# A third raw weight buffer, and another order of the vector work around each step of a gated layer

## The chip, the cores and the metric

The kernel runs on one core of a Trainium2 chip, as one launch. The metric is the device time of one execution in microseconds (us), lower is better. Five engines of the core work here, each on its own instruction stream and strictly in order: PE (TensorE, the matmuls), DVE (VectorE), ACT (ScalarE), POOL (GpSimd) and SP (SyncE), which only issues the transfers. They meet through semaphores, so an instruction that waits holds up everything behind it on its engine.

## The reference

Windowed attention, then a gated layer with SiLU, then a gated layer with a cosine, over 2304 tokens:

```python
attn = softmax(mask(scale * q @ k.T + bias))       # window of 128, 8 heads of 64, 4 sequences of 576
x = concat_heads(attn @ v)                         # [2304, 512]
g = x @ w_gate                                     # 512 x 1536
y = ((g * (1 / (1 + exp(-g)))) * (x @ w_val)) @ w_out   # 1536 x 512
h = y @ w_in2                                      # 512 x 2048
out = (h * cos(h)) @ w_out2                        # 2048 x 512
```

The five weight matrices come as 64-bit floats, q, k and v as 32-bit floats.

## The kernel before

Each matmul operand is held as a high and a low part whose sum is the number, and a product is three matmuls (`mm3`: high·high, high·low, low·high; lines L80, L81, L82). Three phases follow one another. The first does the attention and, as filler, the first 384 hidden columns of the first layer. **The second, which the change touches, does the other 1152 hidden columns of the first layer**, and beside that turns 64-bit weights into high and low parts: those of the first layer for its own later use, those of the second layer for the DRAM tensors `wid` and `wod`. The third does the second layer, which is written with seven products in the place of eight for every 2x2 block of tiles and therefore needs sums of weight blocks (`sm`).

The second phase is a loop of 54 steps. A step is a block of 128 hidden columns (f) and a block of 384 tokens (tb). The hidden blocks go in groups: [3], [4, 5], [6, 7], [8, 9], [10, 11], and for every group the loop runs over the six token blocks and, within them, over the blocks of the group. Step k issues on PE `begin(k)`, which is 12 matmuls for the gate, 12 for the value, and `second(k-2)`, 12 matmuls with `w_out` for the step two before: 36 matmuls in all. The gate bank goes through SiLU on ACT (L984) into `s`, DVE multiplies it by the value bank (L986), `split` makes the high part `uh` on ACT (L993) and the low part `ul` on DVE (L994). The four output banks of `second` are added over a group, and after the last block of the group four DVE adds (L1017) empty them into `acc`; they are posted and come out of `flush` in the next step. The output banks come from a pool of five, so with four in use the next group finds one free bank and must wait for an add for each of the other three.

The weight work is the class `Pipe`. It takes 56 raw tiles (128 x 512 numbers of 64 bits, 512 KB each) through these stages: a transfer into a `stage` tile (L91, L96), issued by SP; two ACT scalings of its upper and lower words (L909, L910), in `scalar`; three DVE operations on the bits (L871, L872, L873) and a POOL add (L875), in `vector`, after which the stage tile is free; then an ACT cast to the high part and a POOL subtract for the low part (L926 and L927 for the first layer, L946 and L947 for the stash, which goes out to DRAM by L952 and L954 from `start`). Tiles of the kind "b" also need four DVE operations for the sums (L891 to L894). Nothing decides the order at run time: every engine's stream is the order in which this loop writes it. In `load` a tile's transfer is written as soon as the add of the tile two before it has been:

```python
while len(self.stages) < min(len(self.todo), self.added + 2):
    self.stages.append(self.todo[len(self.stages)][2]())
```

In a step the order is: `split(k-1)`, `flush` (the bank-emptying adds), `start`, `vector` for the tiles scaled in the step before, `load`, `begin(k)`, then `scalar`, then `second(k-2)`. `scalar` begins one tile, in three steps of ten two.

Of the kernel before, what the change touches and what calls it, by code (L numbers as in the profile page):

```python
# [9 lines left out]
F32 = mybir.dt.float32  # L10
F32R = mybir.dt.float32r
U32 = mybir.dt.uint32
AF = mybir.ActivationFunctionType
ALU = mybir.AluOpType
# [14 lines left out]
def kernel(  # L29
# [12 lines left out]
    nc = tc.nc  # L42
# [20 lines left out]
    xs, cv = ExitStack(), ExitStack()  # L63
    x_pool = xs.enter_context(tc.tile_pool(name="xhl", bufs=1, reuse_waits="tile"))
    wa2_p = ctx.enter_context(tc.tile_pool(name="wa2", bufs=3, side="right", reuse_waits="tile"))
    wa_p = cv.enter_context(tc.tile_pool(name="wa", bufs=6, side="right", reuse_waits="tile"))
    stage_p = cv.enter_context(tc.tile_pool(name="stage", bufs=2, side="right", reuse_waits="tile"))
    cvt = ExitStack()
    conv_p = cvt.enter_context(tc.tile_pool(name="conv", bufs=2, side="right", reuse_waits="tile"))

    xh = x_pool.tile([128, KD, NT], F32R, name="xh")
# [4 lines left out]
    def f32(ap):  # L76
        return ap.bitcast(F32)
# [5 lines left out]

    wide = w_gate.dtype != F32

    def load_stage(src, f, column):
        st = stage_p.tile([128, 512, 2 if wide else 1], U32 if wide else F32, tag="st", name="st")
        src = src.bitcast(U32) if wide else src
        if column:
            n = src.shape[1] // (src.shape[1] // (256 if wide else 128))  # L90
            nc.sync.dma_start(  # L91
                out=st.rearrange("p (k c) t -> p k (c t)", k=KD),
                in_=src[:, f * n:(f + 1) * n].rearrange("(k p) c -> p k c", p=128),
            )
        else:
            nc.sync.dma_start(out=st.rearrange("p c t -> p (c t)"), in_=src[f * 128:(f + 1) * 128, :])  # L96
        return st
# [99 lines left out]
    def flush():  # L197
        for _ in range(len(post)):
            post.popleft()()
# [624 lines left out]
    class Pipe:  # L824
# [3 lines left out]
        def __init__(self):  # L828
            self.todo = []
            for i in range(1, len(groups1)):  # L830
                new = []
                for f in groups1[i]:
                    pool = wa_p if i % 2 else (wa2_p if f == groups1[i][0] else wb_p)
                    for nm, src, col in (("g", w_gate, True), ("v", w_val, True), ("o", w_out, False)):
                        new.append(("w", (i, nm, f), lambda src=src, f=f, col=col: load_stage(src, f, col), pool))
                old = self.stash(2 * i - 4) + self.stash(2 * i - 3) if i > 1 else []
                self.todo += old[:4] + new + old[4:]
            self.todo += self.stash(6) + self.stash(7)
            self.stages, self.begun, self.ct = [], 0, {}
            self.added = self.done = 0  # L840
            self.logic, self.sums, self.parts, self.outs = [], [], deque(), []
            self.kept, self.freed = {}, set()

        def stash(self, p):
            def col(f):
                return lambda: load_stage(w_in2, f, True)

            def row(f):
                return lambda: load_stage(w_out2, f, False)
            return [("a", p, col(2 * p), None), ("b", p, col(2 * p + 1), None),  # L850
                    ("o", 2 * p, row(2 * p), None), ("o", 2 * p + 1, row(2 * p + 1), None)]

# [6 lines left out]
            self.outs = []  # L859

        def load(self):
            while len(self.stages) < min(len(self.todo), self.added + 2):
                self.stages.append(self.todo[len(self.stages)][2]())

        def vector(self):
            for n in self.logic:
                kind, key = self.todo[n][:2]
                st, ct = self.stages[n], self.ct[n]
                if wide:
                    ti = ct.bitcast(U32)  # L870
                    nc.vector.tensor_scalar(ct, ct, LEAST_HIGH, GREATEST_HIGH, ALU.max, ALU.min)  # L871
                    nc.vector.tensor_scalar(ti, ti, 3, None, ALU.logical_shift_left)  # L872
                    nc.vector.scalar_tensor_tensor(out=ti, in0=st[:, :, 1], scalar=0x80000000, in1=ti,  # L873
                                                   op0=ALU.bitwise_and, op1=ALU.bitwise_or)
                    nc.gpsimd.tensor_tensor(out=ti, in0=ti, in1=st[:, :, 0], op=ALU.add)  # L875
                self.added += 1
                self.stages[n] = None
                if kind == "b":
                    self.sums.append((n, 1))
                else:  # L880
                    self.parts.append((n, 0))
            self.logic = []
            later = []
            for n, wait in self.sums:
                if wait:
                    later.append((n, 0))
                    continue
                p = self.todo[n][1]
                a, b = self.kept.pop(p), self.ct[n]
                m = stash_m.tile([128, 4, 256], F32, tag="sm", name="sm")  # L890
                nc.vector.tensor_tensor(out=m[:, 1], in0=b[:, 0:256], in1=b[:, 256:512], op=ALU.add)  # L891
                nc.vector.tensor_tensor(out=m[:, 2], in0=a[:, 0:256], in1=b[:, 0:256], op=ALU.subtract)
                nc.vector.tensor_tensor(out=m[:, 0], in0=m[:, 1], in1=a[:, 0:256], op=ALU.subtract)
                nc.vector.tensor_tensor(out=m[:, 3], in0=a[:, 256:512], in1=m[:, 0], op=ALU.subtract)  # L894
                self.freed.add(n - 1)
                self.kept[n] = m
                self.parts.extendleft([(n, 3), (n, 2), (n, 1)])
            self.sums = later

        def scalar(self, count, ready):  # L900

# [13 lines left out]
            used = 0  # L915
            for _ in range(len(self.parts)):
                n, part = self.parts.popleft()
                kind, key, _, pool = self.todo[n]
                if kind == "w" and not ready(key[0]) or kind != "w" and used == 4:
                    self.parts.append((n, part))  # L920
                    continue
                ct = self.ct[n]
# [11 lines left out]
                if kind == "o":  # L934
                    d = wod[key]
                elif part in (1, 2):
                    src = self.kept[n][:, 2 * part - 2:2 * part].rearrange("p s c -> p (s c)")
                    d = wid[key][:, 2 * part:2 * part + 2]
                elif part == 3:
                    src, w, d = ct[:, 256:512], 256, wid[key][:, 6]  # L940
                else:
                    d = wid[key][:, 0:2]
                    self.kept[key] = ct
# [45 lines left out]
    def split(k):  # L989
        u = state[k]  # L990
        hi = u_p.tile([128, BW], F32R, tag="uh", name="uh")
        lo = u_p.tile([128, BW], F32R, tag="ul", name="ul")
        nc.scalar.copy(out=hi, in_=u)  # L993
        nc.vector.tensor_tensor(out=lo, in0=u, in1=f32(hi), op=ALU.subtract)  # L994
        state[k] = (hi, lo)

    out_ps = {}

# [93 lines left out]
    nc.sync.dma_start(out=acc[:, :, NT - HT:], in_=y1d[:, :, NT - HT:].rearrange("k p t -> p k t"))  # L1092
    fa.close()
    cvt.close()
    ct_p = cv.enter_context(tc.tile_pool(name="cs", bufs=5, side="right", reuse_waits="tile"))
    stash_m = cv.enter_context(tc.tile_pool(name="sm", bufs=1, side="right", reuse_waits="tile"))
    stash_s = cv.enter_context(tc.tile_pool(name="ss", bufs=4, side="right", reuse_waits="tile"))
    s_p2 = sb.enter_context(tc.tile_pool(name="s2", bufs=3, reuse_waits="tile"))
    u_p = sb.enter_context(tc.tile_pool(name="u", bufs=2, reuse_waits="tile"))

    K = len(steps)
    RATEP = 1.3
    begins = {}
    for k, (i, tb, f) in enumerate(steps):
        begins.setdefault(i, k)
    CLOSE = begins[LAST] + 2 * len(groups1[LAST]) + 1
    xt_ops = []

    def work(k, count):
        pipe.start()  # L1110
        pipe.vector()
        pipe.load()
        return lambda: pipe.scalar(count, lambda i: k >= begins[i - 1] + 2)

    for k in range(K + 1):
        if k < K:
            i, tb, f = steps[k]
            while not all((i, nm, f) in weights for nm in "gvo"):
                work(k, 1)()
        if 0 <= k - 1 < K:  # L1120
            split(k - 1)
        flush()
        if k == CLOSE:
            while not pipe.idle():
                work(k, 2)()
            cv.close()
            xta = pre.enter_context(tc.tile_pool(name="xta", bufs=1, side="right", reuse_waits="tile"))
            wsp[0] = pre.enter_context(tc.tile_pool(name="ws", bufs=7, side="right", reuse_waits="tile"))
            load_ws(7)
        if k == CLOSE + 1:  # L1130
            xt_ops = make_xt(0, xta, acc[:, :, 0:SB])
        after = work(k, int((k + 1) * RATEP) - int(k * RATEP)) if k < CLOSE else None
        if k < K:
            begin(k)
        if after:
            after()
        for op in xt_ops[:4]:
            op()
        xt_ops = xt_ops[4:]
        if 0 <= k - 2 < K:  # L1140
            second(k - 2)
# [199 lines left out]
```

## Time and profile before

| | us |
|---|---|
| device time, median of 3 executions | 1170.75 (1166.32 to 1173.18) |
| the profiled execution, device time | 1169.83 |
| its span | 1168.1 |
| first phase, up to the first multiply of the second phase that follows a wait for a raw tile | 312.17 |
| second phase from there to the end of its weight work (44 steps) | 409.37 |
| rest of the second phase, to its last multiply (8 steps) | 50.40 |
| third phase | 396.16 |

The profiled execution is 0.92 us (0.1%) faster than the median and 1.7 us longer than its span. Engine times are busy times within a stretch; the granted clock of PE is a share of its full speed of 2.4 GHz, and a PE that is busy at half clock still counts as busy. Waits are idle times of an engine, put down to what ended them.

### The profile page before, as it was taken

What the parts mean: (1) busy time and instruction counts of PE and PEld (TensorE: products, weight loads), DVE (VectorE), ACT (ScalarE), POOL (GpSimd) and SP (SyncE); (2) the same over time, 40 slices, a digit from 0 to 9 for tenths busy, and PEclk for the clock granted to TensorE, in tenths of its full rate; (3) what the DMA queues carried; (4) which work ended last, traced back from release to release, by engine and by line L of the source; (5) the groups of instructions that cost most, each with busy time, mean ns of one, the idle gap of its engine ahead of it and who ended that gap; (6) DMA issues with size and microseconds to landing.
All of it is one profiled execution on the core that took longest, in us unless ns stands there. A gap on an engine that the chain in (4) does not pass through costs nothing. (4 is left out here: it accounts for less than half of the span.)

```text
span 1168.1 us, 17563 instructions
## 1 busy us (share of the span) xinstructions
PE 1037.0 (89%) x5796; PEld 971.0 (83%) x5796; DVE 752.5 (64%) x1632; ACT 646.4 (55%) x1438; POOL 475.4 (41%) x553
## 2 busy tenths in 40 slices
PE   7989999999867787588687779999999999999998
PEld 5689999999767777587687679988989999998996
DVE  5997877762256565556555656467976688666664
ACT  5989998852232323333343333328767777677663
POOL 5776656653132434343453443103432243222221
PEclk9999999999888888788798799998999999999999
DMA  5542333122613415523542456037666756666652
GB/s 137 151 94 47 86 82 81 46 91 82 214 54 108 135 55 171 172 82 95 174 154 57 154 172 213 28 133 256 189 202 230 221 182 193 189 213 218 191 165 89
DMA packets 145690, 163.68 MB, mean 140 GB/s; under 512 B 64704, under 2 KB 106688, under 8 KB 145344
## 3 DMA queue, kind: packets, MB, share of 16 engines
q1 hardware_dynamic: 145600, 162.57, 45.0%
q8 instruction: 46, 0.75, 0.3%
q14 instruction: 44, 0.36, 0.1%
HBM read 126.88 MB, written 35.65 MB: 139 GB/s over the span
## 5 line engine op out<-in xcount | busy, mean ns | idle before, releaser
L1191 POOL TENSOR_TENSOR r<-r,c 128x384 f32<-128x384 f32 x96 | 104.3, 1086 | 266.2 <-ACT r L1189 179.5
L994 DVE TENSOR_TENSOR ul<-s,uh 128x384 fp32r<-128x384 f32 x54 | 54.8, 1014 | 187.0 <-ACT uh L993 187.0
L80 PE MATMUL l<-uh,wh 128*128 128x384 f32 x216 | 85.1, 394 | 93.2 <-DVE acc L1017 93.2
L909 ACT ACTIVATE cs<-st 128x512 f32<-128x512 f32 x56 | 37.4, 668 | 217.8 <-DMA st<-in_moe_w_out_dram 94.6
L80 PE MATMUL pm<-xh,wh 128*128 128x384 f32 (+1 forms) x452 | 154.6, 342 | 2.0 <-ACT s L984 1.5
L81 PE MATMUL pm<-xl,wh 128*128 128x384 f32 (+1 forms) x452 | 148.5, 328 | 0.0
L82 PE MATMUL pm<-xh,wl 128*128 128x384 f32 (+1 forms) x452 | 147.8, 327 | 0.0
L875 POOL TENSOR_TENSOR cs<-cs,st 128x512 uint32<-128x512 uint32 x56 | 74.7, 1334 | 154.6 <-DVE cs L873 138.2
L80 PEld LDWEIGHTS l<-uh,wh 128*128 128x128 f32 x216 | 46.8, 217 | 100.3 <-DVE acc L1017 100.3
L81 PE MATMUL l<-wo,hh 128*128 128x512 f32 x288 | 113.2, 393 | 0.0
L80 PE MATMUL l<-wo,hh 128*128 128x512 f32 x288 | 113.2, 393 | 0.0
L82 PE MATMUL l<-wo,hl 128*128 128x512 f32 x288 | 112.9, 392 | 0.0
L1073 PE MATMUL pm<-xh,ws 128*128 128x384 f32 x318 | 107.5, 338 | 0.0
L1071 PE MATMUL pm<-xh,ws 128*128 128x384 f32 x318 | 107.5, 338 | 0.0
L1072 PE MATMUL pm<-xl,ws 128*128 128x384 f32 x318 | 107.4, 338 | 0.0
L581 POOL TENSOR_SCALAR e<-e,st 128x256 f32<-128x256 f32 (+1 forms) x144 | 68.7, 488 | 69.5 <-DVE st L576 35.1
L80 PEld LDWEIGHTS pm<-xh,wh 128*128 128x128 f32 x452 | 89.1, 197 | 3.3 <-ACT s L984 2.6
L81 PEld LDWEIGHTS pm<-xl,wh 128*128 128x128 f32 x452 | 88.6, 196 | 0.0
L82 PEld LDWEIGHTS pm<-xh,wl 128*128 128x128 f32 x452 | 87.8, 194 | 0.0
L81 PE MATMUL l<-ul,wh 128*128 128x384 f32 x216 | 82.0, 380 | 0.0
L82 PE MATMUL l<-uh,wl 128*128 128x384 f32 x216 | 82.0, 380 | 0.0
L1181 ACT ACTIVATE a<-c 128x384 f32<-128x384 f32 x96 | 49.9, 519 | 55.9 <-DVE c L1207 55.9
(199 smaller groups left out, 2963.2 us busy)
## 6 DMA issues: line engine op xcount, KB each, us to landing
ws<-wid SPq DMA_DIRECT2D x168, 256.0 KB, 2.8
wo<-wod SPq DMA_DIRECT2D x48, 512.0 KB, 4.9
st<-in_moe_w_out_dram SPq DMA_DIRECT2D x28, 512.0 KB, 3.6
st<-in_moe_w_in_dram SPq DMA_DIRECT2D x16, 512.0 KB, 3.7
st<-in_moe_w_gate_dram SPq DMA_DIRECT2D x12, 512.0 KB, 3.6
st<-in_moe_w_val_dram SPq DMA_DIRECT2D x12, 512.0 KB, 3.8
wid<-sh SPq DMA_DIRECT2D x24, 256.0 KB, 2.5
wid<-sl SPq DMA_DIRECT2D x24, 256.0 KB, 2.5
```

What stands on the lines that cost most here:

```text
L80: nc.tensor.matmul(out=ps, lhsT=ah, rhs=bh, start=start, stop=False)
L81: nc.tensor.matmul(out=ps, lhsT=ah, rhs=bl, start=False, stop=False)
L82: nc.tensor.matmul(out=ps, lhsT=al, rhs=bh, start=False, stop=stop)
L581: nc.gpsimd.tensor_scalar(e[:, :w], e[:, :w], st[:, 6 + m:7 + m], 1.0, ALU.mult, ALU.mult)
L875: nc.gpsimd.tensor_tensor(out=ti, in0=ti, in1=st[:, :, 0], op=ALU.add)
L909: nc.scalar.activation(out=ct, in_=st[:, :, 1].bitcast(F32), func=AF.Abs, scale=65536.0)
L994: nc.vector.tensor_tensor(out=lo, in0=u, in1=f32(hi), op=ALU.subtract)
L1071: nc.tensor.matmul(out=o, lhsT=wh, rhs=xh_, start=start and kk == 0, stop=False, skip_group_check=True)
L1072: nc.tensor.matmul(out=o, lhsT=wh, rhs=xl_, start=False, stop=False, skip_group_check=True)
L1073: nc.tensor.matmul(out=o, lhsT=wl, rhs=xh_, start=False, stop=kk == 1, skip_group_check=True)
L1181: nc.scalar.activation(out=a, in_=h, func=AF.Copy, scale=INV2PI, bias=MAGIC)
L1191: nc.gpsimd.tensor_tensor(out=r, in0=r, in1=h, op=ALU.mult)
```

## The change

There are four edits. (1) The raw stage has three buffers (`stage2`, opened where the old stage and the `conv` pool close) and `load` runs up to three tiles ahead of the adds; the stash pool `ss` goes from four buffers to three for each of its two tags, and at most three stash parts are cast in a step. (2) `scalar`, `vector` and `load` are written in this order behind `begin(k)`, so a tile's DVE operations follow its scalings in the same step, behind the step's multiply; the sums of a "b" tile are the first thing in the next step's `vector`. (3) `split` returns its low part, which is written behind `flush`: the bank-emptying adds stand ahead of it. (4) Two tiles are begun in steps with k % 6 equal to 0 or 2 (from step 6), one in all others.

```diff
@@ Pipe
-            while len(self.stages) < min(len(self.todo), self.added + 2):
+            while len(self.stages) < min(len(self.todo), self.added + 3):
                 self.stages.append(self.todo[len(self.stages)][2]())
         def vector(self):
+            while self.sums:
+                n = self.sums.popleft()
+                a, b = self.kept.pop(self.todo[n][1]), self.ct[n]
+                m = self.kept["m", n] = stash_m.tile([128, 4, 256], F32, tag="sm", name="sm")
...
+                self.parts.extendleft([(n, 3), (n, 2), (n, 1)])
             for n in self.logic:
...
-                if kind == "w" and not ready(key[0]) or kind != "w" and used == 4:
+                if kind == "w" and not ready(key[0]) or kind != "w" and used == 3:
@@ split
         nc.scalar.copy(out=hi, in_=u)
-        nc.vector.tensor_tensor(out=lo, in0=u, in1=f32(hi), op=ALU.subtract)
         state[k] = (hi, lo)
+        return lambda: nc.vector.tensor_tensor(out=lo, in0=u, in1=f32(hi), op=ALU.subtract)
@@ pools of the loop
+    stage2 = cv.enter_context(tc.tile_pool(name="stage2", bufs=3, side="right", reuse_waits="tile"))
-    stash_s = cv.enter_context(tc.tile_pool(name="ss", bufs=4, side="right", reuse_waits="tile"))
+    stash_s = cv.enter_context(tc.tile_pool(name="ss", bufs=3, side="right", reuse_waits="tile"))
@@ the loop
-    def work(k, count):
-        pipe.start()
-        pipe.vector()
-        pipe.load()
-        return lambda: pipe.scalar(count, lambda i: k >= begins[i - 1] + 2)
+    def prepare(k, count):
+        pipe.scalar(count, lambda i: k >= begins[i - 1] + 2)
+        pipe.vector()
+        pipe.load()
+    pipe.load()
...
-        if 0 <= k - 1 < K:
-            split(k - 1)
+        late = split(k - 1) if 0 <= k - 1 < K else None
         flush()
+        if late:
+            late()
...
-        after = work(k, int((k + 1) * RATEP) - int(k * RATEP)) if k < CLOSE else None
+        if k < CLOSE:
+            pipe.start()
         if k < K:
             begin(k)
-        if after:
-            after()
+        if k < CLOSE:
+            prepare(k, 2 if i and k % 2 == 0 and k % 6 != 4 else 1)
```

DVE in step 20 (`ul` of step 19 up to the multiply of step 20), the kernel before:

```order
L994 TENSOR_TENSOR ul<-s,uh 128x384
L1017 TENSOR_TENSOR acc<-l_5698,acc 128x384
L1017 TENSOR_TENSOR acc<-l_5702,acc 128x384
L1017 TENSOR_TENSOR acc<-l_5706,acc 128x384
L1017 TENSOR_TENSOR acc<-l_5710,acc 128x384
L871 TENSOR_SCALAR cs<-cs 128x512
L872 TENSOR_SCALAR cs<-cs 128x512
L873 SCALAR_TENSOR_TENSOR cs<-st,cs 128x512
L871 TENSOR_SCALAR cs<-cs 128x512
L872 TENSOR_SCALAR cs<-cs 128x512
L873 SCALAR_TENSOR_TENSOR cs<-st,cs 128x512
L986 TENSOR_TENSOR s<-s,pm 128x384
```

The same engine and place in the changed kernel, from the end of step 19 into step 20 (its line 980 is the multiply, 989 the low part, 1011 the bank-emptying add, 881 to 883 the operations on a raw tile):

```order
L881 TENSOR_SCALAR cs<-cs 128x512
L882 TENSOR_SCALAR cs<-cs 128x512
L883 SCALAR_TENSOR_TENSOR cs<-st,cs 128x512
L1011 TENSOR_TENSOR acc<-l_5694,acc 128x384
L1011 TENSOR_TENSOR acc<-l_5698,acc 128x384
L1011 TENSOR_TENSOR acc<-l_5702,acc 128x384
L1011 TENSOR_TENSOR acc<-l_5706,acc 128x384
L989 TENSOR_TENSOR ul<-s,uh 128x384
L980 TENSOR_TENSOR s<-s,l_5805 128x384
L881 TENSOR_SCALAR cs<-cs 128x512
L882 TENSOR_SCALAR cs<-cs 128x512
L883 SCALAR_TENSOR_TENSOR cs<-st,cs 128x512
```

The four adds moved from behind `ul` to ahead of it, and the raw tiles from ahead of the multiply to behind it; ahead of the adds there now stands the raw tile of the step before.

SP around steps 18 to 21, the kernel before (the stash parts of the "b" tile 21, then of the next two, with the raw loads between them):

```order
L952 DMA wid_3867<-sh 128x2x256
L952 DMA wid_3867<-sl 128x2x256
L952 DMA wid_3867<-sh 128x2x256
L952 DMA wid_3867<-sl 128x2x256
L954 DMA wid_3867<-sh 128x256
L954 DMA wid_3867<-sl 128x256
L954 DMA wod_3877<-sh 128x512
L954 DMA wod_3877<-sl 128x512
L91 DMA st<-in_moe_w_val_dram 128x4x256
L954 DMA wod_3878<-sh 128x512
L954 DMA wod_3878<-sl 128x512
L96 DMA st<-in_moe_w_out_dram 128x1024
```

SP at the same stash parts in the changed kernel (946 and 948 are the stores):

```order
L91 DMA st<-in_moe_w_val_dram 128x4x256
L96 DMA st<-in_moe_w_out_dram 128x1024
L91 DMA st<-in_moe_w_gate_dram 128x4x256
L946 DMA wid_3867<-sh 128x2x256
L946 DMA wid_3867<-sl 128x2x256
L946 DMA wid_3867<-sh 128x2x256
L946 DMA wid_3867<-sl 128x2x256
L948 DMA wid_3867<-sh 128x256
L948 DMA wid_3867<-sl 128x256
L91 DMA st<-in_moe_w_val_dram 128x4x256
L96 DMA st<-in_moe_w_out_dram 128x1024
L948 DMA wod_3877<-sh 128x512
```

The loads of the same weights stand further ahead in the queue, and the stores of a step stand behind the loads of the step before.

## Rows read from the trace of the kernel before

**Rows 1.** The page: busy time by engine, its share of the span, instructions.

```profile
PE 1037.0 (89%) x5796; PEld 971.0 (83%) x5796; DVE 752.5 (64%) x1632; ACT 646.4 (55%) x1438; POOL 475.4 (41%) x553
```

**Rows 2.** Stretches: length, busy (count) PE, PEld, DVE, ACT, POOL; clock; DMA share; GB/s.

```profile
312.17:721.54 409.37, 314.75 (x1559) 306.32 (x1558) 239.36 (x383) 138.54 (x268) 167.75 (x128) 0.87 0.39 126
721.54:771.94 50.40, 50.40 (x290) 50.40 (x289) 23.75 (x40) 13.16 (x23) 7.58 (x4) 1.00 0.23 74
```

**Rows 3.** DVE timeline, the multiplies of steps 1, 45 and 53: start, length.

```profile
312.17 0.55 DVE L986 TENSOR_TENSOR s<-s,pm 128x384 f32<-128x384 f32 x1
...
721.54 0.56 DVE L986 TENSOR_TENSOR s<-s,pm 128x384 f32<-128x384 f32 x1 [0.30 <-PE pm L82]
...
771.94 0.56 DVE L986 TENSOR_TENSOR s<-s,l 128x384 f32<-128x384 f32 x1 [3.12 <-PE l L82]
```

**Rows 4.** Waits of 312.17 to 721.54: total, times, longest.

```profile
DVE ul L994 <- ACT uh L993: 165.0, 44, 6.9
...
PE l L80 <- DVE acc L1017: 92.1, 21, 10.3
```

**Rows 5.** Timeline of 615 to 625: start, length, idle before.

```profile
615.47 1.31 POOL L875 TENSOR_TENSOR cs<-cs,st 128x512 uint32<-128x512 uint32 x1 [1.55 <-DVE cs L873]
616.81 0.34 SPq L96 DMA_DIRECT2D st<-in_moe_w_out_dram  x1
620.51 0.66 ACT L909 ACTIVATE cs<-st 128x512 f32<-128x512 f32 x1 [5.45 <-DMA st<-in_moe_w_out_dram]
...
622.12 0.52 ACT L993 CAST uh<-s 128x384 fp32r<-128x384 f32 x1
...
622.68 1.39 DVE L994 TENSOR_TENSOR ul<-s,uh 128x384 fp32r<-128x384 f32 x1 [6.82 <-ACT uh L993]
623.99 1.94 DVE L1017 TENSOR_TENSOR acc<-l,acc 128x384 f32<-128x384 f32 x4
...
624.59 0.69 PE L80 MATMUL l<-uh,wh 128*128 128x384 f32 x1 [5.04 <-DVE acc L1017]
```

**Rows 6.** Groups of 312.17 to 721.54: busy, mean ns, idle before and its releasers.

```profile
L909 ACT ACTIVATE cs<-st 128x512 f32<-128x512 f32 x54 | 36.1, 668 | 207.8 <-DMA st<-in_moe_w_out_dram 94.6 <-DMA st<-in_moe_w_in_dram 67.9 <-DMA st<-in_moe_w_val_dram 28.6
...
L994 DVE TENSOR_TENSOR ul<-s,uh 128x384 fp32r<-128x384 f32 x44 | 49.2, 1118 | 165.0 <-ACT uh L993 165.0
L872 DVE TENSOR_SCALAR cs<-cs 128x512 uint32<-128x512 uint32 x55 | 39.1, 711 | 1.9
L871 DVE TENSOR_SCALAR cs<-cs 128x512 f32<-128x512 f32 x55 | 31.6, 575 | 0.0
L892 DVE TENSOR_TENSOR sm<-cs 128x256 f32<-128x256 f32 x8 | 12.2, 1524 | 0.0
```

**Rows 7.** Single lines, same stretch: shortest, median, longest ns.

```profile
L994 DVE TENSOR_TENSOR ul<-s,uh x44: 558/1236/1604, 313.3 to 719.9; 128x384 fp32r<-128x384 f32 x44
L871 DVE TENSOR_SCALAR cs<-cs x55: 410/415/1535, 314.2 to 715.8; 128x512 f32<-128x512 f32 x55
L872 DVE TENSOR_SCALAR cs<-cs x55: 426/428/1426, 314.6 to 716.2; 128x512 uint32<-128x512 uint32 x55
L873 DVE SCALAR_TENSOR_TENSOR cs<-st,cs x56: 691/693/694, 311.6 to 716.7; 128x512 uint32<-128x512 uint32 x56
```

**Rows 8.** Timeline, a POOL subtract and the `ul` that began during it.

```profile
599.64 1.28 POOL L947 TENSOR_TENSOR sl<-cs,sh 128x512 fp32r<-128x512 f32 x1 [3.32 <-issue]
...
599.96 1.38 DVE L994 TENSOR_TENSOR ul<-s,uh 128x384 fp32r<-128x384 f32 x1 [4.55 <-ACT uh L993]
```

**Rows 9.** PE timeline: the first matmul after a short wait, the second after a long one.

```profile
589.57 0.44 PE L80 MATMUL l<-uh,wh 128*128 128x384 f32 x1 [1.26 <-DVE acc L1017]
...
625.08 0.53 PE L81 MATMUL l<-ul,wh 128*128 128x384 f32 x1
```

**Rows 10.** Transfers of the stretch: count, KB each, median us to landing.

```profile
st<-in_moe_w_in_dram SPq DMA_DIRECT2D x16, 512.0 KB, 3.7
wid<-sh SPq DMA_DIRECT2D x24, 256.0 KB, 2.5
```

More of the change, by code (lines that the diff above doesn't have):

```diff
@@ L66 @@
     wa_p = cv.enter_context(tc.tile_pool(name="wa", bufs=6, side="right", reuse_waits="tile"))
-    stage_p = cv.enter_context(tc.tile_pool(name="stage", bufs=2, side="right", reuse_waits="tile"))
     cvt = ExitStack()
+    stage_p = cvt.enter_context(tc.tile_pool(name="stage", bufs=2, side="right", reuse_waits="tile"))
     conv_p = cvt.enter_context(tc.tile_pool(name="conv", bufs=2, side="right", reuse_waits="tile"))
@@ L84, with load_stage @@
     wide = w_gate.dtype != F32
-    def load_stage(src, f, column):
-        st = stage_p.tile([128, 512, 2 if wide else 1], U32 if wide else F32, tag="st", name="st")
+    def load_stage(src, f, column, pool=None):
+        st = (pool or stage_p).tile([128, 512, 2 if wide else 1], U32 if wide else F32, tag="st", name="st")
         src = src.bitcast(U32) if wide else src
@@ L834, in __init__ @@
                     for nm, src, col in (("g", w_gate, True), ("v", w_val, True), ("o", w_out, False)):
-                        new.append(("w", (i, nm, f), lambda src=src, f=f, col=col: load_stage(src, f, col), pool))
+                        new.append(("w", (i, nm, f), lambda src=src, f=f, col=col: load_stage(src, f, col, stage2), pool))
                 old = self.stash(2 * i - 4) + self.stash(2 * i - 3) if i > 1 else []
@@ L840, in __init__ @@
             self.added = self.done = 0
-            self.logic, self.sums, self.parts, self.outs = [], [], deque(), []
+            self.logic, self.sums, self.parts, self.outs = [], deque(), deque(), []
             self.kept, self.freed = {}, set()
@@ L845, in col @@
             def col(f):
-                return lambda: load_stage(w_in2, f, True)
+                return lambda: load_stage(w_in2, f, True, stage2)
             def row(f):
-                return lambda: load_stage(w_out2, f, False)
+                return lambda: load_stage(w_out2, f, False, stage2)
             return [("a", p, col(2 * p), None), ("b", p, col(2 * p + 1), None),
@@ L861, in load @@
         def load(self):
-            while len(self.stages) < min(len(self.todo), self.added + 2):
+            while len(self.stages) < min(len(self.todo), self.added + 3):
                 self.stages.append(self.todo[len(self.stages)][2]())
         def vector(self):
+            while self.sums:
+                n = self.sums.popleft()
+                a, b = self.kept.pop(self.todo[n][1]), self.ct[n]
+                m = self.kept["m", n] = stash_m.tile([128, 4, 256], F32, tag="sm", name="sm")
+                nc.vector.tensor_tensor(out=m[:, 1], in0=b[:, 0:256], in1=b[:, 256:512], op=ALU.add)
+                nc.vector.tensor_tensor(out=m[:, 2], in0=a[:, 0:256], in1=b[:, 0:256], op=ALU.subtract)
+                nc.vector.tensor_tensor(out=m[:, 0], in0=m[:, 1], in1=a[:, 0:256], op=ALU.subtract)
+                nc.vector.tensor_tensor(out=m[:, 3], in0=a[:, 256:512], in1=m[:, 0], op=ALU.subtract)
+                self.freed.add(n - 1)
+                self.parts.extendleft([(n, 3), (n, 2), (n, 1)])
             for n in self.logic:
-                kind, key = self.todo[n][:2]
+                kind = self.todo[n][0]
                 st, ct = self.stages[n], self.ct[n]
@@ L878, in vector @@
                 if kind == "b":
-                    self.sums.append((n, 1))
+                    self.sums.append(n)
                 else:
@@ L882, in vector @@
             self.logic = []
[L883 to L898, printed above, removed]
         def scalar(self, count, ready):
@@ L936, in scalar @@
                 elif part in (1, 2):
-                    src = self.kept[n][:, 2 * part - 2:2 * part].rearrange("p s c -> p (s c)")
+                    src = self.kept["m", n][:, 2 * part - 2:2 * part].rearrange("p s c -> p (s c)")
                     d = wid[key][:, 2 * part:2 * part + 2]
@@ L1101 @@
     K = len(steps)
-    RATEP = 1.3
     begins = {}
@@ L1118 @@
             while not all((i, nm, f) in weights for nm in "gvo"):
-                work(k, 1)()
-        if 0 <= k - 1 < K:
-            split(k - 1)
+                pipe.start()
+                prepare(k, 1)
+        late = split(k - 1) if 0 <= k - 1 < K else None
         flush()
+        if late:
+            late()
         if k == CLOSE:
             while not pipe.idle():
-                work(k, 2)()
+                pipe.start()
+                prepare(k, 2)
             cv.close()
@@ L1131 @@
             xt_ops = make_xt(0, xta, acc[:, :, 0:SB])
-        after = work(k, int((k + 1) * RATEP) - int(k * RATEP)) if k < CLOSE else None
+        if k < CLOSE:
+            pipe.start()
         if k < K:
             begin(k)
-        if after:
-            after()
+        if k < CLOSE:
+            prepare(k, 2 if i and k % 2 == 0 and k % 6 != 4 else 1)
         for op in xt_ops[:4]:
```

## The prediction

> **What bounds the kernel now.** I read the busy times first, then a cut into stretches, then the waits of the worst stretch, then one wait in the timeline. PE is the busiest engine, at 89% of the span [rows 1], but that share hides where it is not. The second phase, from the multiply of step 1 at 312.17 to that of step 45 at 721.54, takes 409.37 us for 44 steps, 9.30 us a step, and in it PE is busy for 314.75 us at a mean clock of 0.87 [rows 2]. The eight steps from 45 to 53 issue the same 36 matmuls each, but no weight work any more: (771.94 - 721.54) / 8 = 6.30 us a step [rows 3], with PE busy throughout at full clock [rows 2]. So 6.30 us is what PE needs, 44 steps of it are 277.2 us, and 132.2 us of the stretch are loss. The loss has two parts: PE idle, 409.37 - 314.75 = 94.6 us, and busy time above the full-speed need, 314.75 - 277.2 = 37.6 us, which the clock accounts for. Of the idle time 92.1 us, in 21 waits, end with a bank-emptying add on DVE [rows 4].
>
> The adds take only 1.94 us for four. They are late because of what stands ahead of them: `ul` waits for `uh` on ACT in every one of the 44 steps, 165.0 us in all [rows 4], and `uh` stands behind the scalings of a raw tile, which wait 207.8 us for transfers [rows 6]. One round shows it [rows 5]: the POOL add of a tile ends at 616.8, SP issues the load into the freed buffer at 616.81, ACT can scale it at 620.51 after 5.45 us of idle, then come the cast and `uh` at 622.12, `ul` at 622.68, the adds at 623.99, and PE goes on at 624.59 after 5.04 us without work. With two buffers, a load waits for the add of the tile two before it. The transfer (3.7 us, median [rows 10]) has to fit between that add and the scaling, and in a step that begins two tiles, and in the step behind it, it does not.
>
> **The change part by part.** No instruction is added or removed: 56 tiles, 44 steps, as many casts and transfers. All of it is order.
>
> *The third buffer* makes a load wait for the add of the tile three before. In the new step a tile is scaled behind the SiLU, some 3 us into the step (24 of PE's 36 matmuls stand ahead of the multiply, so the multiply comes 2/3 x 6.30 = 4.2 us in). Its DVE operations take 0.41 + 0.43 + 0.69 = 1.5 us undisturbed [rows 7], the POOL add 1.31 us [rows 5]. For one tile a step the add ends by about 4.2 + 0.55 + 1.5 + 1.3 = 7.6 us, or by 11.4 where three POOL subtracts of 1.28 us [rows 8] stand ahead of it; the load then lands 0.3 + 3.7 us later, at 15.4. The tile three further on is due at 3 us into the second or third step behind, that is at 15.6 or 21.9. So the raw wait goes to about nothing in most steps and is marginal where two tiles are begun two steps apart. I take the 207.8 us of raw waits as gone but for the allowance below.
>
> *The adds ahead of `ul`* no longer wait for `uh`. They now stand behind the raw tile of the step before. That step is always an odd one with a single tile where the adds are of a pair (a pair ends in odd steps, so its adds come three steps on, in even ones, and the second tile is begun in even steps too). That tile is done at 4.2 + 0.55 + 1.5 = 6.3 us, as the next step begins, 8.1 with the sums (1.5 us for the longest of them, rows 6, and some 0.4 us blocked or not). PE needs the first emptied bank only behind its 24 other matmuls and the one free bank, 4.2 + 0.5 us into that step. That leaves some 2 to 4 us, so a DVE that lags a little costs nothing.
>
> *The multiply ahead of the raw tile* gives PE its `s` banks back earlier and makes `uh` earlier; what hides the tile's 1.5 us is the 2.1 us of `second` on PE. Without that cover it would cost the same 1.5 us in a step. *One stash buffer less and three parts in place of four* cost nothing in POOL or ACT time; what they can cost is a wait (below). *The new rhythm* begins 61 tiles' worth of places up to step 46, as before, and all 56 tiles are done before step 47. The last phase, the first phase and the transfer wait of step 0 (it ends before 312.17) stay.
>
> *What DVE has to carry.* It is busy 239.36 us in the stretch [rows 2], 5.44 a step, already near 6.30. Part of this is blocking. An `ul` takes 558 ns at least and 1118 on average [rows 6, 7], and the one that began 0.32 us into a POOL subtract took 1.38 us and ended 0.42 us behind it [rows 8]: it sat out that instruction. Such time is 44 x 0.56 = 24.6 us for `ul`, 55 x 0.165 = 9.1 for L871 and 55 x 0.285 = 15.7 for L872, 49.4 in all, so DVE undisturbed is 190.0 us. From below: the blocking stays as it is, 239 us, under PE's 277.2. From above: every `ul` takes its longest 1.604 us, every L871 1.535 and every L872 1.426 [rows 7], which adds 44 x 1.05 + 56 x 1.12 + 56 x 1.00 = 165 us: 355 us, 8.07 a step. POOL is busy 167.75 us [rows 2], 41% of the stretch now and 58% if it shrinks to 290 us. Blocking in that proportion is 49.4 x 58 / 41 = 70 us, DVE 260 us, 5.9 a step. That is nearer to the lower end, and PE stays the bound, without much room.
>
> The Trainium skill (SBUF — State Buffer, Who interferes with whom) says that VectorE and GpSimd share a port pair which the one that starts first holds for its whole instruction, while the other fully blocks. The 1.38 us above agrees. The rule speaks against squeezing the same DVE and POOL work into fewer microseconds: taken at its worst it gives the 355 us, and a time of 1115.5 us, where blocking in proportion gives no loss at all.
>
> *The sum.* Outside the stretch nothing moves: 1169.83 - 409.37 = 760.5 us. With 277.2 us for the stretch the time is 1037.7 us; this is the floor. I add an allowance: one short stall in each of the 14 steps that begin two tiles, 1.26 us as the wait at 589.57, behind which the matmuls are fast again [rows 9] (behind a wait of 5 us they take 0.53 us): 17.6 us. The stretch becomes 295 us, 6.70 a step, and the time 760.5 + 294.8 = 1055.3, so 1055 us. The profiled execution lies 0.9 us below the median of the runs, well inside their spread of 7 us.
>
> **The rivals.**
>
> *DVE becomes the bound.* For it speaks the 5.44 us a step at today's pace; against it that much of it is blocking which a later start can also miss. With 355 us the time is 760.5 + 355 = 1115.5; half way from the forecast's stretch, at 325 us, it is 1085.
>
> *The stash waits for itself.* The three stash buffers come free when their stores land; the stores now stand on SP behind the loads of the step before, which wait for POOL adds, which stand behind that step's subtracts. A step with three parts followed by one with two or three would then take a store issue and landing of 0.3 + 2.5 [rows 10], a cast as long as that of `uh`, 0.52 [rows 5], three subtracts of 1.28 [rows 8] and two adds of 1.31 [rows 5]: 9.8 us, 3.5 above 6.30. In the changed order there are 8 such pairs: 28 us, so 1055 + 28 = 1083 us. Against it speaks that PE has a spare bank of `s` and about a step of slack in `uh`.
>
> *The ring only turns differently.* The add of a tile stands later in the step and behind the subtracts; if that eats the third buffer's lead, raw waits stay as they are: 1170 us, no change.
>
> *Slower.* The raw tile's operations now stand on DVE in the step of their scaling, so a late transfer holds the multiply's successor, the adds and `ul` directly. Today 207.8 us of raw waits cost 132.2 us, since a part passes beside the path. If all of it stood on the path, the stretch would be 277.2 + 207.8 = 485 us and the time 1245.5. It decides once more than 132 us of raw waits, 64% of today's, remain and nothing hides them. Against it is the third buffer's lead of a step.
>
> **How the numbers follow.** The forecast has a chance of 0.65 (1038 to 1075 us), DVE as the bound 0.17 (1075 to 1116), the stash 0.09 (about 1083), no effect 0.05, slower 0.04. The range from 1038 to 1105 us takes in the forecast's case, the stash and two thirds of DVE's, 0.85 in all; below the floor there is nothing to win. A measurement of this kernel tells about 0.5% from no change. Faster 0.91, the same 0.05, slower 0.04.
>
> **What would show it.** If right: steps 2 to 44 at 6.3 to 7.0 us between multiplies, PE's waits for the adds below 25 us from 92.1, the waits of the scalings for transfers below 50 us from 207.8, `ul` no longer followed by late adds, and a PE clock of 0.95 or more in the stretch. If DVE is the bound, it is busy for nearly all of the stretch, with `ul` and L872 (now 882) well above their present means. If the stash binds, the casts of L946 wait for stores. It would be wrong if scalings still sit idle for transfers for more than 100 us, or PE still waits in long pieces of 5 us and the clock falls with them.

## The result, and the profile after

The changed kernel takes 1066.34 us, median of 4 executions (1061.86 to 1067.96), against 1168.98 us of the kernel before, timed beside it (4 executions, 1166.32 to 1173.18): a ratio of 0.9113, with a 95% interval from 0.9071 to 0.9154. That is 103 us less, where 115 were forecast. The profiled execution has a span of 1065.4 us.

The page, as in [rows 1]: PE is now busy for 95% of the span, DVE for 72%.

```profile
PE 1010.7 (95%) x5796; PEld 949.8 (89%) x5796; DVE 762.2 (72%) x1632; ACT 647.6 (61%) x1438; POOL 485.1 (46%) x553
```

The second phase between the same two multiplies (step 1 to step 45) and the steps behind it, columns as in [rows 2]:

```profile
311.70:621.92 310.22, 289.98 (x1569) 286.21 (x1568) 249.13 (x382) 141.51 (x269) 176.50 (x128) 0.95 0.51 163
621.92:671.06 49.14, 49.14 (x283) 49.14 (x282) 23.86 (x40) 13.13 (x23) 7.73 (x4) 1.00 0.24 80
```

Nearly all of the gain is in this stretch: 409.37 - 310.22 = 99.2 us, of the 102.7 us by which the spans differ. It is 33.0 us above the 277.2 that PE needs: 310.22 - 289.98 = 20.2 us idle, and 289.98 - 277.2 = 12.8 us of busy time above the need at full clock; the mean granted clock is 0.95.

The waits of this stretch in the changed kernel (its lines 903, 940, 978, 987, 989 and 1011 are the former 909, 946, 984, 993, 994 and 1017), columns as in [rows 4]:

```profile
ACT sh L940 <- DMA wid<-sh: 62.9, 21, 9.0
...
DVE ul L989 <- ACT uh L987: 47.3, 14, 6.5
...
ACT sh L940 <- DMA wod<-sh: 22.3, 5, 9.2
...
PE l L80 <- ACT s L978: 12.1, 4, 5.1
PE l L80 <- DVE acc L1011: 10.9, 4, 4.2
```

and its scalings, as in [rows 6]:

```profile
L903 ACT ACTIVATE cs<-st 128x512 f32<-128x512 f32 x54 | 36.0, 666 | 17.7 <-DMA st<-in_moe_w_gate_dram 6.6 <-DMA st<-in_moe_w_out_dram 4.1 <-DMA st<-in_moe_w_val_dram 4.1
```

The scalings wait 17.7 us for raw tiles in place of 207.8, and PE waits 10.9 us for bank-emptying adds in place of 92.1. In the place of the raw tiles stands a new wait: the casts of the stash (L940) sit 62.9 + 22.3 = 85.2 us behind stores of their own earlier contents. One of them in the timeline, with the same columns as [rows 5]:

```profile
354.13 2.86 POOL L941 TENSOR_TENSOR sl<-sm,sh 128x512 fp32r<-128x512 f32 x2 [0.31 <-ACT sh L940]
...
360.54 3.08 POOL L885 TENSOR_TENSOR cs<-cs,st 128x512 uint32<-128x512 uint32 x2
...
362.19 0.34 SPq L96 DMA_DIRECT2D st<-in_moe_w_out_dram  x1
...
363.64 0.37 SPq L91 DMA_DIRECT2D st<-in_moe_w_gate_dram  x1
...
364.07 0.50 SPq L946 DMA_DIRECT2D wid<-sh  x1
...
370.07 0.62 ACT L940 CAST sh<-cs 128x512 fp32r<-128x512 f32 x1 [9.01 <-DMA wid<-sh]
...
372.46 0.51 ACT L987 CAST uh<-s 128x384 fp32r<-128x384 f32 x1
372.87 0.48 ACT L978 ACTIVATE s<-l 128x384 f32<-128x384 f32 x1
...
373.41 0.69 PE L80 MATMUL l<-xh,wh 128*128 128x384 f32 x1 [3.58 <-ACT s L978]
```

POOL ends the two adds of step 8 at about 362.1 and at 363.6. SP stands at the load behind each (362.19, 363.64), and only then comes to the stores of the three parts cast in that step, from 364.07, although the subtracts of the first two had ended at 357.0. The next cast needs one of these three buffers: ACT is idle for 9.01 us, 3.0 of them before the store is issued and 6.0 behind that; `uh` and the SiLU stand behind the cast, and PE idles for 3.58 us because the SiLU has not emptied its bank.

### The profile page after: what moved, and what is told of

The parts are those of the page before. It is cut to its first block, busy times and chain, and to the rows that moved or that the text cites. A ratio compares the mean times of both kernels' runs of the same rounds, so it can differ in the third digit from the quotient of the medians.

```text
span 1065.4 us, 17549 instructions
## 1 busy us (share of the span) xinstructions
PE 1010.7 (95%) x5796; PEld 949.8 (89%) x5796; DVE 762.2 (72%) x1632; ACT 647.6 (61%) x1438; POOL 485.1 (46%) x553
## 4 chain that ended last, share of the span: by engine, by line
PE 45%; DMA 5%; POOL 3%; DVE 3%; issue 2%; ACT 1%; SPq 1%; POOLq 0%; ACTq 0%; DVEq 0%
PE l L80 8%; PE l L81 8%; PE l L82 8%; PE pm L1065 5%; PE pm L1066 5%; PE pm L1067 5%; POOL cs L885 2%; PE pm L80 2%; PE pm L82 2%; PE pm L81 1%; DMA wid<-sh 1%; POOL sl L941 1%; DMA wod<-sl 1%; DMA wid<-sl 1%; DMA ws<-wid 1%
## 5 line engine op out<-in xcount | busy, mean ns | idle before, releaser
L80 PE MATMUL pm<-xh,wh 128*128 128x384 f32 (+1 forms) x452 | 152.2, 337 | 2.3 <-ACT s L978 2.3
L885 POOL TENSOR_TENSOR cs<-cs,st 128x512 uint32<-128x512 uint32 x56 | 81.8, 1465 | 64.6 <-DVE cs L883 50.3
L80 PEld LDWEIGHTS pm<-xh,wh 128*128 128x128 f32 x452 | 86.6, 192 | 3.2 <-ACT s L978 3.2
L80 PE MATMUL l<-uh,wh 128*128 128x384 f32 x216 | 75.0, 347 | 11.0 <-DVE acc L1011 10.9
L989 DVE TENSOR_TENSOR ul<-s,uh 128x384 fp32r<-128x384 f32 x54 | 42.7, 791 | 52.9 <-ACT uh L987 52.8
L1184 DVE SCALAR_TENSOR_TENSOR r<-a,r 128x384 f32<-128x384 f32 x96 | 74.4, 775 | 3.3
L1186 ACT ACTIVATE r<-r 128x384 f32<-128x384 f32 x96 | 50.3, 524 | 40.4 <-DVE r L1184 40.4
L82 PE MATMUL l<-uh,wl 128*128 128x384 f32 x216 | 74.2, 343 | 0.0
L81 PE MATMUL l<-ul,wh 128*128 128x384 f32 x216 | 74.2, 343 | 0.0
```

The lines of the kernel that those rows point to most:

```text
L80: nc.tensor.matmul(out=ps, lhsT=ah, rhs=bh, start=start, stop=False)
L81: nc.tensor.matmul(out=ps, lhsT=ah, rhs=bl, start=False, stop=False)
L82: nc.tensor.matmul(out=ps, lhsT=al, rhs=bh, start=False, stop=stop)
L1184: nc.vector.scalar_tensor_tensor(out=r, in0=a, scalar=-C2, in1=r, op0=ALU.mult, op1=ALU.add)
L1186: nc.scalar.activation(out=r, in_=r, func=AF.Abs)
```

## The experiments

(The expectations give the casts' waits of the changed kernel as 81 us, for one of the two groups of casts; with both it is the 85.2 us above.) All were timed beside the kernel before. "Stretch" is the time from the multiply of step 1 to that of step 45 in the profiled execution.

| kernel | time, us | ratio to before (95%) | stretch, us |
|---|---|---|---|
| the kernel before | 1169 | | 409.37 |
| the changed kernel | 1066.34 | 0.9113 (0.9071 to 0.9154) | 310.22 |
| 1: two raw buffers | 1113.75 | 0.9516 (0.9485 to 0.9548) | 355.72 |
| 2: third raw buffer alone | 1066.69 | 0.9125 (0.9107 to 0.9143) | 306.86 |
| 3: low part ahead of the adds | 1090.21 | 0.9329 (0.9299 to 0.9359) | 330.50 |
| 4: stores ahead of loads | 1036.87 | 0.8870 (0.8855 to 0.8885) | 280.44 |
| 5: four buffers for high parts | 1064.58 | 0.9109 (0.9088 to 0.9130) | 307.38 |
| 6: third buffer, adds ahead | 1036.97 | 0.8876 (0.8857 to 0.8894) | 280.26 |
| 7: 4 with the low part ahead | 1044.95 | 0.8935 (0.8908 to 0.8962) | 287.65 |
| 8: before, three stash buffers | 1165.31 | 0.9970 (0.9954 to 0.9985) | |
| 9: old rhythm | 1060.42 | 0.9075 (0.9054 to 0.9097) | |
| 10: 4 with the old rhythm | 1034.68 | 0.8856 (0.8833 to 0.8880) | |

Theory A, the prediction's, is that the raw tile's early transfer wins the time and the order makes room for it. Rival B is that the order on DVE wins it.

**1. Two raw buffers in the new order.**

```diff
-    stage2 = ... bufs=3        min(len(self.todo), self.added + 3)
+    stage2 = ... bufs=2        min(len(self.todo), self.added + 2)
```

> The changed kernel with two raw buffers in place of three, all else as changed. Theory A (the raw tile's early transfer is what the change wins): the scalings wait for transfers for more than 120 us again in the second phase (17.7 in the changed kernel, 207.8 before), and the time is 1120 to 1180 us. Rival B (the order on the vector engine wins it, adds ahead of the low part and raw tiles behind the multiply): at most 20 us are lost, 1066 to 1086 us.

The scalings of this kernel, as in [rows 6], and below them PE's wait for the adds, as in [rows 4]:

```profile
L903 ACT ACTIVATE cs<-st 128x512 f32<-128x512 f32 x54 | 36.0, 667 | 151.8 <-DMA st<-in_moe_w_out_dram 82.8 <-DMA st<-in_moe_w_in_dram 30.4 <-DMA st<-in_moe_w_gate_dram 20.5
```

```profile
PE l L80 <- DVE acc L1011: 49.0, 11, 7.4
```

The raw waits are back, as A says, but the time missed A's span on the low side and B's on the high side: without any third buffer the rest of the change is 56 us faster than the kernel before. Neither theory alone holds.

**2. The third raw buffer alone, in the old order** (with it the smaller stash of the change).

```diff
-    stage_p ... bufs=2         self.added + 2     name="ss", bufs=4     used == 4
+    stage2 ... bufs=3          self.added + 3     name="ss", bufs=3     used == 3
```

> The kernel before with the third raw buffer alone (one stash buffer less, three stash parts a step; old order, old rhythm). Theory A: most of the 103 us come from the buffer, the time is 1070 to 1100 us and the scalings wait under 80 us for transfers. Rival B: the buffer alone brings less than a third, 1135 to 1170 us, since the low part still stands ahead of the bank-emptying adds and the raw tile's operations still come a step late.

The scalings of this kernel:

```profile
L909 ACT ACTIVATE cs<-st 128x512 f32<-128x512 f32 x54 | 36.1, 668 | 38.9 <-DMA st<-in_moe_w_out_dram 21.0 <-DMA st<-in_moe_w_in_dram 13.1 <-DMA st<-in_moe_w_gate_dram 4.3
```

and its waits:

```profile
DVE ul L994 <- ACT uh L993: 68.7, 44, 2.5
PE l L80 <- DVE acc L1017: 21.0, 14, 3.7
ACT sh L946 <- DMA wid<-sh: 3.8, 4, 1.3
```

The buffer alone gives as much as the whole change, 3 us below A's span. What it leaves is of another kind: its casts wait 3.8 us for stores, not 85, but `ul` still waits in all 44 steps ahead of the adds, and PE waits 21.0 us for these. So with the third buffer the other edits together add nothing; experiments 4, 6 and 9 take them apart.

**3. The low part back ahead of the adds.**

```diff
-        flush()
         if late:
             late()
+        flush()
```

> The changed kernel with the low part back ahead of the bank-emptying adds. Theory A: with the raw tiles in time the high part is early, the low part waits little, and 0 to 10 us are lost, 1066 to 1076 us. Rival B: the adds again stand behind every late high part, and 20 us or more are lost; the waits for stores on the scalar engine (81 us in the changed kernel) would then pass to the matmuls.

Two of its waits:

```profile
ACT sh L940 <- DMA wid<-sh: 58.4, 20, 9.4
PE l L80 <- DVE acc L1011: 41.5, 8, 9.4
```

24 us are lost, B's answer: with the low part first, PE waits 41.5 us for the adds in place of 10.9. ACT waits for stores about as long as in the changed kernel; with the adds first, less of its lateness reaches PE.

**4. Stores ahead of loads.** A step's stores only wait for its subtracts, which stand ahead of its adds on POOL, so they can be written before the loads.

```diff
     def prepare(k, count):
         pipe.scalar(count, lambda i: k >= begins[i - 1] + 2)
         pipe.vector()
+        pipe.start()
         pipe.load()
```

> The changed kernel with the stash stores of a step written ahead of that step's raw loads on the transfer queue, in place of behind them in the next step. Theory C (of the 33 us above the matmuls' need the casts' waits for stash stores are the cause): the casts' waits fall from 81 us to under 30, and the time falls to 1045 to 1057 us. Rival D (the vector engine, blocked by GpSimd, is the cause): the casts' waits fall but the time stays at 1062 to 1070 us. Rival E (the loads behind the stores come too late): waits of the scalings above 50 us and 1070 us or more.

The stretch of this kernel, as in [rows 2]:

```profile
308.76:589.20 280.44, 276.44 (x1562) 274.83 (x1561) 256.75 (x382) 143.16 (x269) 178.09 (x128) 0.99 0.57 185
```

and two of its waits:

```profile
ACT sh L940 <- DMA wid<-sh: 5.4, 7, 2.0
...
PE l L80 <- DVE acc L1011: 4.0, 5, 1.5
```

This is theory C, beyond its span: 29 us less than the changed kernel, and a stretch of 6.37 us a step. DVE is busy for 256.75 of 280.44 us, 92%, and does not hold PE up, so D is out; the scalings wait 3.0 us for transfers, so E is out too. The same stores, at SP in this kernel, go out ahead of the loads of step 8:

```profile
352.39 0.51 SPq L946 DMA_DIRECT2D wid<-sh  x1
...
358.56 0.33 SPq L96 DMA_DIRECT2D st<-in_moe_w_out_dram  x1
```

**5. A fourth buffer for the high parts**, with a pool of its own for the three low ones.

> The changed kernel with four buffers for the stash's high parts in place of three (low parts stay at three; stores stay behind the next loads). Theory C (the casts wait because the high part's buffer is still being stored, and the stores are late on the queue): a fourth buffer lets the first cast behind a step of three parts go on, the casts' waits for stores fall from 85 us to 30 to 60 and the time to 1045 to 1062 us. Rival F (only the queue's order counts, every buffer is late): no change, 1063 to 1069 us.

```profile
ACT sh L940 <- DMA wid<-sh: 50.4, 11, 10.1
...
POOL sl L941 <- DMA wid<-sl: 13.7, 4, 5.8
...
ACT sh L940 <- DMA wod<-sh: 11.2, 6, 3.2
```

F's answer by the time, which stays. The casts' waits do fall, from 85.2 to 50.4 + 11.2 = 61.6 us, close to what C expected, and bring nothing. POOL still waits for its three low-part buffers, so this leaves open what a fourth pair would do; that one was not tried.

**6. The third buffer and the adds ahead, in the old place of the raw tiles** (experiment 2 and the edit to `split` and `flush`).

> The third buffer in the old order (1067 us) with the bank-emptying adds ahead of the low part, nothing else. Theory G (what is left there is the 21 us that the matmuls wait for adds, behind a low part that waits for its high part): the waits for adds fall under 10 us and the time to 1040 to 1055 us. Rival H (the adds then stand behind the raw tile's operations or the multiply, and the waits only move): 1060 to 1070 us.

Its stretch, and PE's wait for the adds:

```profile
309.01:589.27 280.26, 276.42 (x1566) 274.15 (x1565) 244.31 (x382) 140.59 (x268) 170.68 (x128) 1.00 0.56 180
```

```profile
PE l L80 <- DVE acc L1017: 3.5, 5, 1.1
```

G, and lower than it said. The raw waits in it are 44.9 us (21.2 + 17.7 + 5.4 + 0.6 by their four sources), more than in the changed kernel, and cost PE nothing. This kernel differs from the changed one only by the place of the raw tiles (edit 2) and by the rhythm. Putting the raw tiles behind the multiply is thus what makes the changed kernel slower, by 29 us, or by 23 with the old rhythm in both (experiment 9), and it wins nothing that the third buffer has not won. That it costs this through the stores is what experiments 4 and 10 show, which get the time back by the stores' place alone.

**7. Experiment 4 with the low part ahead of the adds.**

> The changed kernel with stores ahead of loads (1037 us) and the low part back ahead of the bank-emptying adds. If the 24 us that this edit cost without the stores moved were due to the scalar engine being late for stores, nothing is left to lose: 1036 to 1042 us. If the order of the adds is worth something by itself, 1050 to 1062 us.

```profile
PE l L80 <- DVE acc L1011: 8.1, 5, 2.0
```

Between the two answers: 8 us are lost, and the wait for the adds is 8.1 us in place of 4.0. So of the 24 us of experiment 3 some 16 go with ACT being late for stores, and 8 remain without that.

**8. The kernel before with three stash buffers and three parts**, the control for experiment 2.

> The kernel before with three stash buffers and three stash parts a step and its two raw buffers, a control for the third raw buffer alone. If the gain of that kernel is the raw buffer's: 1165 to 1180 us. If fewer parts a step help by themselves: below 1155 us.

At 0.997 (0.9954 to 0.9985) the smaller stash gives 2 to 5 us; the rest of the gain of experiment 2, 97 us or more, is the raw buffer's.

**9 and 10. The old rhythm**, in the changed kernel and in experiment 4.

```diff
-            prepare(k, 2 if i and k % 2 == 0 and k % 6 != 4 else 1)
+            prepare(k, int((k + 1) * 1.3) - int(k * 1.3))
```

> The changed kernel with the old rhythm (a second tile in three steps of ten, from step 0). If the rhythm is bookkeeping: 1060 to 1072 us. If it matters that a second tile falls in even steps, ahead of steps without bank-emptying adds: 1075 us or more.

> The changed kernel with stores ahead of loads (1037 us) and the old rhythm. If the rhythm is bookkeeping: 1035 to 1040 us. If a second tile in an odd step makes the adds late, 1042 us or more, and the matmuls' waits for adds rise from 4 to over 8 us.

The rhythm is bookkeeping. If anything, the old one is a little faster (0.9075 and 0.8856 beside 0.9113 and 0.8870), but the intervals overlap. In experiment 10 PE waits 2.4 us for the adds, not over 8.

## Why the prediction was right, and where its sum was off

**The bound** was read rightly: the loss was in the 44 steps with weight work, and it came from raw transfers through ACT to the adds. The scalings' waits fell to 17.7 us (under 50 forecast), PE's waits for the adds to 10.9 (under 25), the clock rose to 0.95. The steps, at 310.22 / 44 = 7.05 us, lie just above the 6.3 to 7.0 forecast. The floor also holds: with everything out of the way (experiments 4 and 6) the stretch is 280.4 and 280.3 us against 277.2 worked out.

**The third buffer** was to end the raw waits; the prediction gave no edit a share of the gain. Experiments 2 and 8 show that the buffer can carry nearly all of it, and experiment 1 that the other edits have 56 us of it without the buffer.

**The adds ahead of the low part** were said not to wait for `uh` any more and to have 2 to 4 us to spare. Experiments 3, 6 and 7 bear this out and put a price on it: 24, 30 and 8 us. It goes with how long `ul` waits for `uh` where it stands first: 59.4 us in experiment 3, 68.7 in experiment 2 (beside 6) and 3.7 in experiment 7.

**The step that failed** is the one that put the stash's wait for its own stores at nothing in the sum, and kept it as a rival with a chance of 0.09, because a spare bank of `s` and a step of slack in `uh` would cover it. The stores behind the loads are what the changed kernel pays for: its stretch is 310.22 - 280.44 = 29.8 us longer than that of experiment 4, and the casts' waits for stores, which the prediction named as this rival's sign, are there. The slack was too small for a wait of 9 us, as the round at 370.07 shows. Three stash buffers by themselves do not cost it (experiment 2's casts wait 3.8 us); the raw tiles' new place does, through the queue.

The rival's own 28 us came so near partly by luck. They were 8 pairs of steps at 3.5 us, without a loss of clock; measured are 26 waits of casts, and of the 29.8 us 16.2 are idle time of PE (20.2 against 4.0) and 13.5 more busy time (289.98 against 276.44), at a granted clock of 0.95 against 0.99. The price also took 2.5 us for a store to land, and in the changed kernel the median is 4.6 (columns as in [rows 10]):

```profile
wid<-sh SPq DMA_DIRECT2D x24, 256.0 KB, 4.6
```

It is 4.8 in experiment 1, 4.2 in experiment 4 and 3.9 in experiment 6, at DMA shares of 0.45, 0.57 and 0.56, so the share alone does not explain it; why a store lands later was not tested. **The allowance**, 17.6 us for short stalls where two tiles are begun, was mis-sized the other way: 280.4 - 277.2 = 3.2 us is all that is left when the stores are early, and experiment 10 shows no loss from other steps for the second tile. Outside the stretch, where nothing was to move, the time fell from 760.5 to 1067.15 - 310.22 = 756.9 us. With these sizes the sum is 756.9 + 277.2 + 3.2 + 29.8 = 1067.1, the profiled execution. The errors, 29.8 one way and 14.4 and 3.6 the other, partly cancel, so that 1055 came within 12 us of it is in part luck.

**DVE as the bound** did not come true. Its busy time grew with the same operations (256.75 us in experiment 4 against 239.36 in [rows 2]), close to the 260 us worked out from the share of POOL, and PE still ran at its own pace. The working counted no blocking for L873, though; in experiment 4 this operation takes 1021 ns on average in place of 693.

## What to carry to other kernels

When an engine waits for a transfer and others wait for that engine in order, there are two cures: start the transfer earlier, and take what the last engine needs out from behind the waiting one. Try each alone before both together; here the change without its third buffer brought half of the gain and the buffer alone all of it, the buffer and the adds ahead of the low part 132 us, and the raw tiles' new place, bundled with them, took 23 to 29 us back. (The adds ahead alone, with two buffers, were not run.) And when work is moved later in a step, look at the issuing queue too: a transfer that waits for the moved work holds every store written behind it, and the buffers of these stores.

## What the runs showed of the hardware that was not expected

The DVE operation that takes the raw tile and its scaled copy, both in SBUF (L873, 691 to 694 ns in [rows 7]), always kept its time in the kernel before. In the changed kernel, where it can meet a POOL operation, it takes up to 1814 ns:

```profile
L883 DVE SCALAR_TENSOR_TENSOR cs<-st,cs x55: 691/693/1814, 313.7 to 611.1; 128x512 uint32<-128x512 uint32 x55
```

The longest one begins 0.05 us behind a POOL subtract and ends 0.55 us behind the end of it:

```profile
544.51 1.31 POOL L921 TENSOR_TENSOR wl<-cs,wh 128x512 fp32r<-128x512 f32 x1 [0.73 <-ACT wh L920]
544.56 1.81 DVE L883 SCALAR_TENSOR_TENSOR cs<-st,cs 128x512 uint32<-128x512 uint32 x1
```

The Trainium skill (SBUF — State Buffer, Who interferes with whom) says that a vector operation with two inputs in SBUF contends with a GpSimd operation that reads SBUF; the 1814 ns agree. In experiment 6, with the raw tiles in their old place, the operation stays at 691 to 695 ns. That it never happened before fits with POOL's waiting for this very operation there:

```profile
POOL cs L875 <- DVE cs L873: 138.2, 49, 20.7
```

This was not tested by itself.
